# Batch 0 of a Fourier mixing and gated feed-forward kernel: the mean-frequency row on four column tiles, another order of the first loads, and the places and steps at which the weights are prepared

## The chip, the cores and the metric

The kernel runs on one core of one Trainium2 chip. The metric is the device time in microseconds (us); the median of three runs before is 1972.15 us (1970.73 to 1973.31).

## The reference

`x` is 8 batches of 3008 positions of 256 features, float32. Each batch goes through a two-dimensional Fourier transform of which the real part is kept; every position then goes through a gated feed-forward layer. The three weights arrive as 64-bit floats.

```python
def _attn_ref(x) -> np.ndarray:
    X = np.fft.fft(x, axis=1)
    X = np.fft.fft(X, axis=2)
    return X.real.astype(np.float32)
...
def _moe_ref(x, w_gate, w_val, w_out) -> np.ndarray:
    gate = 1.0 / (1.0 + np.exp(-(x @ w_gate)))
    val = x @ w_val
    return (gate * val @ w_out).astype(np.float32)
```

## The kernel before, in words

**Transform over positions.** The symmetry of the real transform is used: `fold_ops` (L347) adds and subtracts mirrored rows of a batch, and TensorE multiplies the folded rows with a table of cosines or sines (tile `st`, six pieces `q` of 126 rows, halves by `load_table`). Each product group has an even and an odd sum, `ev` and `od`; ScalarE copies `ev` out (L439) and VectorE combines the two (`places`, L444 and L447) into one of three tiles with a column per frequency: `pk` (cosine part), `qk` (sine part), and for batch 0 `ek`, the part E of the one feature in the middle (column HD). In batch 0 that one column is broadcast to all 128 columns of the stationary operand, so that `ek` holds the same row 128 times (`seq_group` with `what` = 2). The other seven batches get E as rows in one go, from `e_sums` (L476): the product has 7 columns, four products stand side by side at 32-column positions of the array, and the rows go to memory (`ed`) and come back broadcast (`e_rows`, tile `ek`).

**Weights.** There are 18 pieces of 512 KB, 256 columns of the gate or value weight or 256 rows of the output weight, in the order `jobs` (L205). A piece is loaded by SyncE's queue into a "raw" place (`weight_load`), taken apart on ScalarE (`weight_parts`, L262 and L263, two operations), joined to float32 on VectorE and GpSimd (`weight_join`, L272, L273, L275, and L277 on GpSimd), and used (`weight_use`). A gate or value piece is multiplied on TensorE with the feature transform `dt` (`merge`, matmuls `ps`), and ScalarE copies the result to `G1`, `G2` (L298, L299); two small transfers put row 0 of `G2` into `ge` (L301). An output piece goes to `WO`; when all that a group `g` needs of it is there, three operations for forming sums of weight blocks are appended to the list `parts_` (`forms`, L304; sums L334 and L337 by `W_SUMS`, copies on ScalarE L341). They write the 15 forms of group `g` in `wf`. Group 0 is formed on GpSimd, groups 1 to 3 on VectorE.

**The main loop** (`for i in range(count)`, L792) runs over 576 steps, one for 128 hidden units of a chunk of 252 frequencies; 12 steps make a chunk. Within a step the code order is the order on every engine, and the engines keep their own order. In step `i`:

- `front_a(i)`: TensorE multiplies `G1` with `pk` into PSUM tile `pf` (4 rows of the trace), in the first N1 steps also `G2` with a tile whose row 0 is E (`e0`, 4 rows);
- `part(i)`: a copy `ae` of `pf`, doubled, on ScalarE (L548); for N1 <= i < 12 instead two operations on VectorE that add E times `ge` (L551);
- `gate_a(i-1)`, `gate_b(i-1)`: sigmoid (ScalarE L567), difference (VectorE L572 or L569), product (VectorE L584), sigmoid (ScalarE L585), product (VectorE L586), and sums of blocks on GpSimd (L590);
- then, if `parts_` holds anything, its first operation, and the joins, parts and uses of weights that the two lists near the end (`pre`, `use`) give for this step; if `parts_` was empty, its first operation comes after them;
- from step 5 on `back((i-5)//3, (i-5)%3)`: 5 products with the forms in `wf` (matmuls `po`, 10 rows). `PRODUCTS` names the form of each: the third product of part 0 needs form 6, the fourth form 10; the first product of part 1 needs form 4. Group 1 is first used in step 8, group 2 in step 11, group 3 in step 14;
- `front_b(i)`: TensorE multiplies `G2` with `qk` into the same `pf` (4 rows).

From step 12 on, E enters by ScalarE's `seed` (L532), which writes `ek` times `ge` to the next `pf`.

Of the kernel before, what the change touches and what calls it, by code (L numbers as in the profile page):

```python
# [7 lines left out]
F32 = mybir.dt.float32  # L8
# [36 lines left out]

NQ = 6
NP = 126  # L50
HP = 64
# [3 lines left out]
              (15, 4, 6, 1)),  # L55
          2: ((11, 8, 11, 0), (12, 8, 12, 0), (9, 5, 9, 0), (10, 10, 5, 0), (16, 2, 11, 0),
              (16, 9, 16, 0))}
W_SUMS = (((1, 3), (5,), 1, 6), ((6, 7), (0, 2), 0, 8), ((4,), (8, 9), 0, 10), ((6,), (2, 3), 1, 12),
          ((0, 2), (1, 3), 0, 14), ((0,), (7,), 1, 16))
W_COPIES = ((2, -1), (0, 1), (4, 1), (5, 1))  # L60

PRODUCTS = ((0, 12), (1, 11), (4, 6), (6, 10), (2, 13), (5, 4), (13, 0),
# [15 lines left out]
def kernel(  # L78
# [10 lines left out]
    nc = tc.nc  # L89
    B, _, _, _, D = xf.shape  # L90
    F = moe_w_gate.shape[1]
    P = 128
# [102 lines left out]
    def table_again():  # L195

        ST[0] = const.tile([P, 2, NQ, NE + NO], F32, name="st", tag="st")
        for t in range(2):
# [3 lines left out]


    assert NPR == 6
    jobs = [(0, 0), (1, 0), (0, 1), (1, 1), (2, 0), (0, 2), (1, 2), (2, 1), (0, 3), (1, 3), (0, 4), (2, 2),  # L205
            (1, 4), (0, 5), (1, 5), (2, 3), (2, 4), (2, 5)]
    RAW, WS = {}, {}
    shared = {}
    KEEP = 10
# [1 line left out]
    def weight_load(j):  # L211


        w, c = jobs[j]
        src = (moe_w_gate, moe_w_val, moe_w_out)[w]
        src = src[2 * c * P : 2 * (c + 1) * P, :] if w == 2 else src[:, c * WC : (c + 1) * WC]
        src = src.rearrange("(c p) f -> p c f", p=P)

        def some(n, pool, tag):

            if tag not in shared:
                shared[tag] = pool.tile([P, n * WC], F32, name=f"w{tag}", tag=tag)
            return shared[tag]

        def home(j):

            if j in (0, 1, 2, 3, 5):
                if j > 2:
                    ws = some(5, pqp, "qk")[:, (j // 5) * 2 * WC : (j // 5 + 1) * 2 * WC]
                    return sp.tile([P, 4 * WC], F32, name="raw", tag="sf"), ws  # L230
                t = hp.tile([P, 6 * WC], F32, name="raw", tag="h")
                return t[:, 0 : 4 * WC], t[:, 4 * WC :]
            if j in (4, 6, 9):
                t = wf[:, {4: 1, 6: 2, 9: 3}[j]].rearrange("p m n -> p (m n)")
                return t[:, 0 : 4 * WC], t[:, 4 * WC : 6 * WC]
            t = some(10, cp, "c")
            if j == 7:
                raw = pqp.tile([P, 4 * WC], F32, name="raw", tag="pk")
                return raw, t[:, 6 * WC : 8 * WC]
            return t[:, 0 : 4 * WC], t[:, 4 * WC : 6 * WC]  # L240

        if j < KEEP:
            raw, ws = home(j)
        else:
            both = some(24, xp, "x4").rearrange("p (i n) -> p i n", n=2 * WC)
            r, i = (j - KEEP) % 3 * 2, 6 + (j - KEEP) % 6
            raw, ws = both[:, r : r + 2].rearrange("p a n -> p (a n)"), both[:, i]
        raw = raw.bitcast(I32).rearrange("p (c f w) -> p c f w", c=2, w=2)
        ws = ws.rearrange("p (c f) -> p c f", c=2)
        WS[j] = ws  # L250
        if src.dtype == F32:
            nc.sync.dma_start(out=ws, in_=src)
        else:
            RAW[j] = raw
            nc.sync.dma_start(out=raw.rearrange("p c f w -> p c (f w)"), in_=src.bitcast(I32))
# [48 lines left out]
    def forms(g):  # L304
# [1 line left out]
        w = [WO[f // 2].rearrange("p f (a h j) -> p f h a j", h=2, j=TB)[:, f % 2]  # L306
             for f in range(3 * g, 3 * g + 3)]
        f = wf[:, g].rearrange("p m (a j) -> p m a j", j=TB)
        engine = nc.vector if g else nc.gpsimd

        def one(i):
            return w[i // 2][:, i % 2] if i < 6 else f[:, i - 6]

# [14 lines left out]
        def sums(lo, hi):  # L328
            for x, y, op, to in W_SUMS[lo:hi]:
                n = max(len(x), len(y))  # L330
                a, b = blocks(x, n), blocks(y, n)
                op = (ALU.subtract, ALU.add)[op]
                if a is not None and b is not None:
                    engine.tensor_tensor(f[:, to - 6 : to - 6 + n], a, b, op=op)  # L334
                else:
                    for i in range(n):
                        engine.tensor_tensor(f[:, to - 6 + i], one(x[i % len(x)]), one(y[i % len(y)]), op=op)  # L337

        def copies():
            for i, (a, sign) in enumerate(W_COPIES):  # L340
# [6 lines left out]
    def fold_ops(b, nq):  # L347
# [58 lines left out]
            first(pool, 2, 3, qs[1])  # L406
            ops += [lambda: half1(qs[0]), lambda: half2(qs[1])]
        for blk, (v, r) in enumerate(parts):
            W[b, blk] = (v[:, :, 0:HD], r[:, :, 0:HD],
                         v[:, :, HD : HD + 1].to_broadcast([v.shape[0], NQ, P]))  # L410
        return ops


# [40 lines left out]

    def seq_start(b):
        PQE[b] = [pqp.tile([P, NK + 1], F32, name=name, tag=name) for name in ("pk", "qk")]
        if not b:
            PQE[b].append(op.tile([P, NK + 1], F32, name="ek", tag="os"))
        for t in PQE[b]:
            nc.vector.memset(t[:, NK:], 0.0)  # L460

# [11 lines left out]
        tt(x8[:, :, 1], x8[:, :, 0], x8[:, :, 2], op=ALU.add)  # L473
        tt(x8[:, :, 3], x8[:, :, 0], x8[:, :, 2], op=ALU.subtract)

    def e_sums():  # L476


        ps = bank("pe", 0)
        m = B - 1  # L480
        at_ = lambda blk, par: slice((2 * blk + par) * TB, (2 * blk + par) * TB + m)
        for q in range(0, NQ, 2):
            for blk in range(2):
                c0, n = ((0, NE), (NE, NO))[blk]
                for par in range(2):
                    mm(ps[at_(blk, par), 0:n], x8[:, :, 1 + 2 * blk, q + par],
                       ST[0][0:NP, 0, q + par, c0 : c0 + n], q == 0, q == NQ - 2)
        er = op.tile([P, NK + 1], F32, name="er", tag="os")[0:m]
        nc.vector.memset(er[:, NK:], 0.0)
        a = evp.tile([P, NE], F32, name="a", tag="a")[0:m]  # L490
        e1 = evp.tile([P, NE], F32, name="a", tag="a")[0:m]
        nc.scalar.copy(a, ps[at_(0, 1), 0:NE])
        nc.scalar.copy(e1[:, 0:NO], ps[at_(1, 0), 0:NO])

        def rest():
            places(er, 0, True, a, ps[at_(0, 0), 0:NE])
            nc.scalar.copy(a[:, 0:NO], ps[at_(1, 1), 0:NO])  # L497
            places(er, 1, False, e1[:, 0:NO], a[:, 0:NO])
            nc.scalar.dma_start(out=ed[1:], in_=er)
        return rest  # L500


# [17 lines left out]
        nc.sync.dma_start(out=EK[i // NFT], in_=ed[b : b + 1, k0 : k0 + n].to_broadcast([P, n]))  # L520

    PF, AP, Z = {}, {}, {}
    N1 = 5

    def seed(i):

# [16 lines left out]
    def part(i):  # L543

        pqe, ks, n, f, _ = cut(i)
        AP[i] = app.tile([P, 2, CH], F32, name="ae", tag="ae")[:, :, 0:n]
        if not N1 <= i < NFT:
            nc.scalar.activation(AP[i], PF[i], AF.Copy, scale=2.0)  # L548
            return
        for g in range(2):  # L550
            nc.vector.scalar_tensor_tensor(out=AP[i][:, g], in0=pqe[2][:, ks],  # L551
                                           scalar=ge[:, g, f : f + 1], in1=PF[i][:, g],
                                           op0=ALU.mult, op1=ALU.add)

# [131 lines left out]
    for j in range(2):  # L686
        weight_load(j)
    load_x(0)
    for _ in load_table(0, NQ // 2):
        pass  # L690
    for j in range(2, 5):
        weight_load(j)
    sines = load_table(1, NQ // 2)
    next(sines)
    for j in range(5, 7):
        weight_load(j)
    next(sines)
    for j in range(7, KEEP):
        weight_load(j)

    def weight_round(*js):
# [11 lines left out]

    e0 = shared["qk"][:, 4 * WC : 4 * WC + CH]
    nc.gpsimd.memset(e0, 0.0)
    other = {(0, 0): (4, None), (0, 1): (4, None), (0, 2): (0, 1), (1, 2): (2, 3)}
    cos = [seq_group(0, blk, what, other.get((blk, what))) for blk in range(2) for what in (0, 2)]
    for i, f in enumerate(fold_ops(0, NQ // 2)):
        f()
        for sums, _, _ in cos:  # L720
            sums(*range(i * NQ // 2, (i + 1) * NQ // 2))
    sin = [seq_group(0, blk, 1, other.get((blk, 1))) for blk in range(2)]
    for i in range(2):
        for sums, _, _ in sin:
            sums(*range(i * NQ // 2, (i + 1) * NQ // 2))
    evacuate = [then for _, then, _ in cos + sin]
    for then, js in zip(evacuate, ((2, 3), (4,), (5,), (6,), (7,), (8,))):
        weight_round(*js)
        then()()
    nc.scalar.dma_start(out=ed[0:1], in_=PQE[0][2][0:1])  # L730
    nc.vector.tensor_copy(e0[0:1], PQE[0][2][0:1, 0:CH])
    weight_parts(9)
    for j in range(KEEP, KEEP + 3):
        weight_load(j)
    weight_use(2)

# [5 lines left out]


    pre, use = {}, {}
    for j, i in enumerate((0, 1, 2, 3, 4, 5, 6, 7, 9), 9):
        if i:
            pre.setdefault(i - 1, []).append(lambda j=j: weight_parts(j))
        pre.setdefault(i, []).insert(0, lambda j=j: weight_join(j))
        if KEEP <= j < len(jobs) - 3:
            at(i, lambda j=j: weight_load(j + 3))  # L750
    for j, i in enumerate((0, 0, 1, 2, 0, 3, 4, 5, 4, 6, 7, 8, 8, 8, 11), 3):
        use.setdefault(i, []).append(lambda j=j: weight_use(j))
    at(N1 - 1, lambda: nc.vector.tensor_copy(PQE[0][1][0:1, 0:CH], PQE[0][2][0:1, 0:CH]))


    i0 = NFT
# [7 lines left out]
    for i, f in enumerate(mirror_tables()):  # L764
        at(2 * i0 - 2 + i, f)
    at(3 * i0, e_fold)
    at(3 * i0 + 4, lambda: e_sums()())
    at(3 * i0 + 6, table_again)
    for i in range(i0, count, i0):
        at(i - 8, lambda i=i: e_rows(i))  # L770

    for b in range(B - 1):
        s0 = b * per
# [97 lines left out]
```

## Time and profile before

| | |
|---|---|
| median of three runs | 1972.15 us |
| profiled execution, its own time | 1973.76 us |
| its span, first to last instruction | 1972.0 us |
| TensorE busy | 1935.8 us, 98% |
| VectorE, ScalarE, GpSimd busy | 1511.7, 1339.5, 1625.0 us |
| mean granted TensorE clock | 0.995 |
| steps 0, 12 and 16 begin (`pf` from `pk`) | 49.02, 107.91, 120.76 us |

A timeline line gives the start, the duration (of all merged instructions together), engine, line, operation, output and inputs, shapes, and in brackets the idle time before it and what ended it. A table of stretches gives the length, then the busy time and the number of instructions of each engine, TensorE's granted clock, the share of the transfer engines and their rate. `PEld` is TensorE's weight load, which lies beside its matmuls. A float32 product is two rows of the trace.

### The profile page before, as it was taken

The page shows a single profiled execution, that of the slowest core. Times are in us where ns is not written, and L with a number is a line of the kernel's source. Part 1 is how long each engine was busy: PE and PEld are TensorE (multiplying, and loading weights), DVE is VectorE, ACT ScalarE, POOL GpSimd, SP SyncE. Part 2 cuts the span into 40 slices and gives each one's busy share as a digit, 9 for nine tenths or more (in the row PEclk, how much of TensorE's full clock was granted, in tenths as well). Part 3 has the DMA queues.
Part 4 walks back from the last instruction along what each step waited for, and adds up shares of the span by engine and source line. Part 5 has one row for each costly group of instructions (what it writes and reads, how often), then busy time and mean ns, then how long its engine had stood idle before and what let it go on. Part 6 is the DMA issues. An engine that isn't in the chain of part 4 may idle for free.

```text
span 1972.0 us, 34403 instructions
## 1 busy us (share of the span) xinstructions
PE 1935.8 (98%) x11252; PEld 1792.4 (91%) x11252; DVE 1511.7 (77%) x3170; ACT 1339.5 (68%) x3108; POOL 1625.0 (82%) x2843
## 2 busy tenths in 40 slices
PE   6999999999999999999999999999999999999997
PEld 4889889999999899998999989999899999999997
DVE  6888778886787677786778867787678776777777
ACT  3567657766777577775777757777577766777775
POOL 3779888997889788996889868998688996777776
PEclk9999999999999999999999999999999999999999
DMA  8363412212022121212012021211210110011011
GB/s 271 86 134 94 138 52 85 51 22 78 14 51 54 17 76 17 72 31 78 14 28 78 14 78 25 47 48 24 78 19 14 21 20 14 14 20 22 14 19 27
DMA packets 171584, 101.41 MB, mean 51 GB/s; under 512 B 133904, under 2 KB 163218, under 8 KB 168602
## 3 DMA queue, kind: packets, MB, share of 16 engines
q1 hardware_dynamic: 169434, 98.64, 20.6%
q8 instruction: 90, 1.47, 0.3%
q10 hardware_dynamic: 1940, 0.56, 0.1%
q14 instruction: 88, 0.72, 0.1%
q0 software_dynamic: 32, 0.00, 0.0%
HBM read 74.45 MB, written 50.18 MB: 63 GB/s over the span
## 4 chain that ended last, share of the span: by engine, by line
PE 95%; DMA 2%; DVE 2%; ACT 1%; issue 0%; POOL 0%; SPq 0%; ACTq 0%; DVEq 0%; POOLq 0%
PE pf L129 49%; PE po L129 41%; PE ev L129 4%; DMA st<-in_stab_dram 1%; PE ps L129 1%; DMA ge<-G 1%; PE od L129 0%; DMA raw<-in_moe_w_val_dram 0%; DMA xr<-in_xf_dram 0%; DVE c L637 0%; DVE ae L551 0%; DVE wf L337 0%; DVE wx L273 0%; ACT z L585 0%; DVE wx L275 0%
## 5 line engine op out<-in xcount | busy, mean ns | idle before, releaser
L590 POOL TENSOR_TENSOR sf<-h 128x168 f32<-128x168 f32 (+1 forms) x960 | 548.8, 590 | 221.6 <-DVE h L586 221.6
L590 POOL TENSOR_TENSOR sf<-h,sf 128x168 f32<-128x168 f32 (+1 forms) x1152 | 657.2, 590 | 60.5 <-DVE h L586 60.5
L129 PE MATMUL pf<-qk,G 128*128 128x252 f32 (+1 forms) x2304 | 582.4, 375 | 3.1 <-DVE ae L551 2.0
L129 PE MATMUL pf<-pk,G 128*128 128x252 f32 (+1 forms) x2304 | 583.4, 376 | 0.0
L586 DVE TENSOR_TENSOR h<-z 128x252 f32<-128x252 f32 (+1 forms) x576 | 299.1, 519 | 356.9 <-ACT z L585 356.6
L532 ACT ACTIVATE pf<-ek,ge 128x252 f32<-128x252 f32 (+1 forms) x1128 | 531.4, 471 | 18.4
L129 PE MATMUL po<-sf,wf 128*128 128x168 f32 (+1 forms) x3072 | 530.1, 305 | 0.0
L548 ACT ACTIVATE ae<-pf 128x504 f32<-128x504 f32 (+1 forms) x569 | 335.0, 589 | 245.6 <-PE pf L129 245.5
L637 DVE TENSOR_TENSOR c<-c 128x168 f32<-128x168 f32 (+1 forms) x949 | 484.3, 541 | 5.5 <-ACT c L614 0.3
L129 PEld LDWEIGHTS pf<-pk,G 128*128 128x128 f32 x2304 | 436.7, 190 | 52.6 <-issue 2.3
L129 PEld LDWEIGHTS po<-sf,wf 128*128 128x128 f32 x3072 | 472.8, 190 | 8.3
L129 PE MATMUL po<-h,wf 128*128 128x168 f32 (+1 forms) x2688 | 477.2, 306 | 1.7 <-ACT a L497 1.6
L129 PEld LDWEIGHTS po<-h,wf 128*128 128x128 f32 x2688 | 428.8, 191 | 19.0 <-ACT a L497 2.0
L129 PEld LDWEIGHTS pf<-qk,G 128*128 128x128 f32 x2304 | 410.2, 190 | 29.2 <-DVE ae L551 2.6
L572 DVE TENSOR_TENSOR z<-ae,pf 128x504 f32<-128x504 f32 (+1 forms) x569 | 377.4, 663 | 21.5 <-ACT h L567 20.9
L567 ACT ACTIVATE h<-pf 128x252 f32<-128x252 f32 (+1 forms) x576 | 217.9, 378 | 164.0 <-PE pf L129 152.9
L585 ACT ACTIVATE z<-z 128x252 f32<-128x252 f32 (+1 forms) x576 | 231.1, 401 | 80.3 <-DVE z L572 60.1
L584 DVE TENSOR_TENSOR h<-h,pf 128x252 f32<-128x252 f32 (+1 forms) x576 | 231.9, 403 | 0.0
L590 POOL TENSOR_TENSOR sf<-sf 128x168 f32<-128x168 f32 (+1 forms) x192 | 111.3, 580 | 15.1
L590 POOL TENSOR_TENSOR sf<-sf,h 128x168 f32<-128x168 f32 (+1 forms) x192 | 106.6, 555 | 0.0
L129 PE MATMUL ev<-st,x 63*128 63x376 f32 (+4 forms) x372 | 98.0, 414 | 8.3 <-DVE x L364 7.8
L129 PEld LDWEIGHTS ev<-st,x 63*128 63x128 f32 (+1 forms) x372 | 66.4, 187 | 36.1 <-DVE x L364 8.2
(120 smaller groups left out, 861.9 us busy)
## 6 DMA issues: line engine op xcount, KB each, us to landing
x<-xr SPq DMA_DIRECT2D x14, 1536.0 KB
out_dram<-os SPq DMA_DIRECT2D x380, 56.0 KB
xr<-in_xf_dram SPq DMA_DIRECT2D x14, 768.0 KB
xr<-in_xf_dram SPq DMA_DIRECT2D x35, 256.0 KB
ek<-ed SPq DMA_DIRECT2D x39, 126.0 KB
out_dram<-os SPq DMA_DIRECT2D x288, 7.0 KB
st<-in_stab_dram SPq DMA_DIRECT2D x4, 1111.9 KB
x<-in_xf_dram SPq DMA_DIRECT2D x2, 1512.0 KB
```

What stands on the lines that cost most here:

```text
L129: nc.tensor.matmul(o, l, r, start=start, stop=stop, skip_group_check=True)
L532: nc.scalar.activation(PF[i][:, g], EK[i // NFT], AF.Copy, scale=ge[:, g, f : f + 1])
L548: nc.scalar.activation(AP[i], PF[i], AF.Copy, scale=2.0)
L567: nc.scalar.activation(H[p][:, fh, 0:n], PF[i][:, 0], AF.Sigmoid)
L572: nc.vector.tensor_tensor(z[:, :, ::-1], AP.pop(i), PF[i], op=ALU.subtract)
L584: nc.vector.tensor_tensor(h[:, fh, 0:n], h[:, fh, 0:n], PF.pop(i)[:, 1], op=ALU.mult)
L585: nc.scalar.activation(z[:, 0], z[:, 0], AF.Sigmoid)
L586: nc.vector.tensor_tensor(h[:, fh, n:], z[:, 0], z[:, 1], op=ALU.mult)
L590: nc.gpsimd.tensor_tensor(block(p, dst), block(p, a), block(p, b), op=(ALU.subtract, ALU.add)[op])
L637: engine.tensor_tensor(t[:, dst * R : (dst + 1) * R], *v, op=(ALU.subtract, ALU.add)[op])
```

## The change

1. **E of batch 0.** `e_sums` gets the number of rows, the column and the batch as arguments and is used for batch 0 too, with one row: 12 products at four column positions take the place of the 12 with the broadcast column. The row goes to memory, and `e_rows(0)` brings it back, broadcast, for VectorE's E part of steps 8 to 11. All later `e_rows` are issued two steps sooner (`i - 10`).
2. **Loads.** The sines' first half is loaded directly behind the cosines, the second half after one weight piece; pieces 3 to 9 follow. The order of pieces (`jobs`) changes: gate and value pieces 0 to 2 come first, then the first two output pieces.
3. **Places.** From piece 10 on there are five raw places where there were three (two of them in a second tile of pool `cp`), and five pieces are loaded ahead of the loop.
4. **Before the loop** only pieces 2 to 4 are prepared (it was 2 to 8); the later joins and uses move into the loop by the two lists.
5. **Forms.** Group 0 is formed on VectorE; `W_SUMS` is in another order, so that the first two operations give what part 0 of `back` needs, and the third gives form 4 for part 1.
6. **N1** goes from 5 to 8: TensorE adds E in three more steps, and VectorE in three fewer.

```diff
-W_SUMS = (((1, 3), (5,), 1, 6), ((6, 7), (0, 2), 0, 8), ((4,), (8, 9), 0, 10), ((6,), (2, 3), 1, 12),
-          ((0, 2), (1, 3), 0, 14), ((0,), (7,), 1, 16))
+W_SUMS = (((1, 3), (5,), 1, 6), ((0,), (7,), 1, 16), ((6,), (2, 3), 1, 12), ((6, 7), (0, 2), 0, 8),
+          ((4,), (8, 9), 0, 10), ((0, 2), (1, 3), 0, 14))
...
-    jobs = [(0, 0), (1, 0), (0, 1), (1, 1), (2, 0), (0, 2), (1, 2), (2, 1), (0, 3), (1, 3), (0, 4), (2, 2),
-            (1, 4), (0, 5), (1, 5), (2, 3), (2, 4), (2, 5)]
+    jobs = [(w, c) for c in range(3) for w in range(2)] + [(2, 0), (2, 1), (0, 3), (1, 3)]
+    jobs += [(0, 4), (1, 4), (2, 2), (0, 5), (1, 5), (2, 3), (2, 4), (2, 5)]
...
-            r, i = (j - KEEP) % 3 * 2, 6 + (j - KEEP) % 6
-            raw, ws = both[:, r : r + 2].rearrange("p a n -> p (a n)"), both[:, i]
+            r, ws = (j - KEEP) % 5, both[:, 6 + (j - KEEP) % 6]
+            if r < 3:
+                raw = both[:, 2 * r : 2 * r + 2].rearrange("p a n -> p (a n)")
+            else:
+                if r == 3:
+                    shared["more"] = cp.tile([P, 10 * WC], F32, name="wm", tag="c")
+                raw = shared["more"][:, (r - 3) * 4 * WC : (r - 2) * 4 * WC]
...
-        engine = nc.vector if g else nc.gpsimd
...
-            W[b, blk] = (v[:, :, 0:HD], r[:, :, 0:HD],
-                         v[:, :, HD : HD + 1].to_broadcast([v.shape[0], NQ, P]))
+            W[b, blk] = v[:, :, 0:HD], r[:, :, 0:HD], v[:, :, HD : HD + 1]
...
-    N1 = 5
+    N1 = 8
...
-            nc.vector.scalar_tensor_tensor(out=AP[i][:, g], in0=pqe[2][:, ks],
+            nc.vector.scalar_tensor_tensor(out=AP[i][:, g], in0=EK[i // NFT],
...
-    for _ in load_table(0, NQ // 2):
-        pass
-    for j in range(2, 5):
-        weight_load(j)
+    list(load_table(0, NQ // 2))
     sines = load_table(1, NQ // 2)
     next(sines)
-    for j in range(5, 7):
-        weight_load(j)
+    weight_load(2)
     next(sines)
-    for j in range(7, KEEP):
+    for j in range(3, KEEP):
         weight_load(j)
...
-    cos = [seq_group(0, blk, what, other.get((blk, what))) for blk in range(2) for what in (0, 2)]
+    cos = [seq_group(0, blk, 0, (2 * blk + 1, 2 * blk + 2)) for blk in range(2)]
...
+    e_row = e_sums(1, lambda blk, q: W[0, blk][2][:, q], 0)
...
-    for then, js in zip(evacuate, ((2, 3), (4,), (5,), (6,), (7,), (8,))):
-        weight_round(*js)
+    for _, then, _ in cos:
         then()()
-    nc.scalar.dma_start(out=ed[0:1], in_=PQE[0][2][0:1])
-    nc.vector.tensor_copy(e0[0:1], PQE[0][2][0:1, 0:CH])
-    weight_parts(9)
-    for j in range(KEEP, KEEP + 3):
+    e_row = e_row()
+    weight_round(2)
+    nc.vector.tensor_copy(e0[0:1], e_row[:, 0:CH])
+    for j, (_, then, _) in zip((3, 4), sin):
+        weight_round(j)
+        then()()
+    weight_parts(5)
+    for j in range(KEEP, KEEP + 5):
         weight_load(j)
     weight_use(2)
...
-    for j, i in enumerate((0, 1, 2, 3, 4, 5, 6, 7, 9), 9):
+    for j, i in enumerate((0, 1, 2, 2, 3, 4, 5, 6, 6, 7, 8, 9, 10), 5):
...
-    for j, i in enumerate((0, 0, 1, 2, 0, 3, 4, 5, 4, 6, 7, 8, 8, 8, 11), 3):
+    for j, i in enumerate((0, 1, 2, 3, 3, 4, 5, 6, 7, 7, 8, 9, 10, 10, 12), 3):
         use.setdefault(i, []).append(lambda j=j: weight_use(j))
-    at(N1 - 1, lambda: nc.vector.tensor_copy(PQE[0][1][0:1, 0:CH], PQE[0][2][0:1, 0:CH]))
+    at(N1 - 1, lambda: nc.vector.tensor_copy(PQE[0][1][0:1, 0:CH], e_row[:, 0:CH]))
...
+    e_rows(0)
     for i in range(i0, count, i0):
-        at(i - 8, lambda i=i: e_rows(i))
+        at(i - 10, lambda i=i: e_rows(i))
```

More of the change, by code (lines that the diff above doesn't have):

```diff
@@ L333, in sums @@
                 if a is not None and b is not None:
-                    engine.tensor_tensor(f[:, to - 6 : to - 6 + n], a, b, op=op)
+                    nc.vector.tensor_tensor(f[:, to - 6 : to - 6 + n], a, b, op=op)
                 else:
                     for i in range(n):
-                        engine.tensor_tensor(f[:, to - 6 + i], one(x[i % len(x)]), one(y[i % len(y)]), op=op)
+                        nc.vector.tensor_tensor(f[:, to - 6 + i], one(x[i % len(x)]), one(y[i % len(y)]), op=op)
         def copies():
@@ L456, in seq_start @@
         PQE[b] = [pqp.tile([P, NK + 1], F32, name=name, tag=name) for name in ("pk", "qk")]
-        if not b:
-            PQE[b].append(op.tile([P, NK + 1], F32, name="ek", tag="os"))
         for t in PQE[b]:
@@ L474, in e_fold, with e_sums @@
         tt(x8[:, :, 3], x8[:, :, 0], x8[:, :, 2], op=ALU.subtract)
-    def e_sums():
+    def e_sums(m, column, b):
         ps = bank("pe", 0)
-        m = B - 1
         at_ = lambda blk, par: slice((2 * blk + par) * TB, (2 * blk + par) * TB + m)
@@ L485, in e_sums @@
                 for par in range(2):
-                    mm(ps[at_(blk, par), 0:n], x8[:, :, 1 + 2 * blk, q + par],
+                    mm(ps[at_(blk, par), 0:n], column(blk, q + par),
                        ST[0][0:NP, 0, q + par, c0 : c0 + n], q == 0, q == NQ - 2)
[L488 to L493, printed above, removed]
-        def rest():
+        def rest():
+            er = op.tile([P, NK + 1], F32, name="er", tag="os")[0:m]
+            nc.vector.memset(er[:, NK:], 0.0)
+            a = evp.tile([P, NE], F32, name="a", tag="a")[0:m]
+            e1 = evp.tile([P, NE], F32, name="a", tag="a")[0:m]
+            nc.scalar.copy(a, ps[at_(0, 1), 0:NE])
+            nc.scalar.copy(e1[:, 0:NO], ps[at_(1, 0), 0:NO])
             places(er, 0, True, a, ps[at_(0, 0), 0:NE])
@@ L498, in rest @@
             places(er, 1, False, e1[:, 0:NO], a[:, 0:NO])
-            nc.scalar.dma_start(out=ed[1:], in_=er)
+            nc.scalar.dma_start(out=ed[b : b + m], in_=er)
+            return er
         return rest
@@ L715 @@
     nc.gpsimd.memset(e0, 0.0)
-    other = {(0, 0): (4, None), (0, 1): (4, None), (0, 2): (0, 1), (1, 2): (2, 3)}
-    cos = [seq_group(0, blk, what, other.get((blk, what))) for blk in range(2) for what in (0, 2)]
+    cos = [seq_group(0, blk, 0, (2 * blk + 1, 2 * blk + 2)) for blk in range(2)]
     for i, f in enumerate(fold_ops(0, NQ // 2)):
@@ L721 @@
             sums(*range(i * NQ // 2, (i + 1) * NQ // 2))
-    sin = [seq_group(0, blk, 1, other.get((blk, 1))) for blk in range(2)]
+    e_row = e_sums(1, lambda blk, q: W[0, blk][2][:, q], 0)
+    sin = [seq_group(0, blk, 1, (None, 1 if blk else None)) for blk in range(2)]
     for i in range(2):
@@ L725 @@
             sums(*range(i * NQ // 2, (i + 1) * NQ // 2))
-    evacuate = [then for _, then, _ in cos + sin]
-    for then, js in zip(evacuate, ((2, 3), (4,), (5,), (6,), (7,), (8,))):
-        weight_round(*js)
+    for _, then, _ in cos:
         then()()
-    nc.scalar.dma_start(out=ed[0:1], in_=PQE[0][2][0:1])
-    nc.vector.tensor_copy(e0[0:1], PQE[0][2][0:1, 0:CH])
-    weight_parts(9)
-    for j in range(KEEP, KEEP + 3):
+    e_row = e_row()
[6 more added lines that the diff above has]
+    for j in range(KEEP, KEEP + 5):
         weight_load(j)
@@ L748 @@
         pre.setdefault(i, []).insert(0, lambda j=j: weight_join(j))
-        if KEEP <= j < len(jobs) - 3:
-            at(i, lambda j=j: weight_load(j + 3))
-    for j, i in enumerate((0, 0, 1, 2, 0, 3, 4, 5, 4, 6, 7, 8, 8, 8, 11), 3):
+        if KEEP <= j < len(jobs) - 5:
+            at(i, lambda j=j: weight_load(j + 5))
+    for j, i in enumerate((0, 1, 2, 3, 3, 4, 5, 6, 7, 7, 8, 9, 10, 10, 12), 3):
         use.setdefault(i, []).append(lambda j=j: weight_use(j))
-    at(N1 - 1, lambda: nc.vector.tensor_copy(PQE[0][1][0:1, 0:CH], PQE[0][2][0:1, 0:CH]))
+    at(N1 - 1, lambda: nc.vector.tensor_copy(PQE[0][1][0:1, 0:CH], e_row[:, 0:CH]))
     i0 = NFT
@@ L766 @@
     at(3 * i0, e_fold)
-    at(3 * i0 + 4, lambda: e_sums()())
+    at(3 * i0 + 4, lambda: e_sums(B - 1, lambda blk, q: x8[:, :, 1 + 2 * blk, q], 1)())
     at(3 * i0 + 6, table_again)
+    e_rows(0)
     for i in range(i0, count, i0):
-        at(i - 8, lambda i=i: e_rows(i))
+        at(i - 10, lambda i=i: e_rows(i))
     for b in range(B - 1):
```

## The prediction

> **What bounds the kernel now.** I read the page first, then the table of stretches for the first 250 us, the timeline by engine and the chain of waits. The page's slices, about 49 us each:
>
> ```profile
> PE   6999999999999999999999999999999999999997
> PEclk9999999999999999999999999999999999999999
> ```
>
> TensorE is the bound from the third slice on, so what the first 120 us lose or win passes to the end one for one. Those stretches:
>
> ```profile
> 70.00:80.00 10.00, 7.95 (x38) 6.17 (x36) 9.63 (x18) 5.28 (x16) 6.96 (x10) 1.00 0.53 163
> 80.00:90.00 10.00, 9.43 (x50) 8.44 (x51) 9.56 (x19) 3.58 (x11) 8.99 (x12) 1.00 0.22 54
> 90.00:100.00 10.00, 10.00 (x58) 9.26 (x56) 9.21 (x20) 4.28 (x13) 7.21 (x11) 1.00 0.19 45
> 100.00:110.00 10.00, 8.00 (x37) 7.34 (x36) 9.45 (x20) 4.23 (x13) 7.33 (x12) 0.83 0.54 179
> ```
>
> The third busy column is VectorE: 9.2 to 9.6 of 10 us. In steps 5 to 11 VectorE is as tight as TensorE. The timeline of TensorE:
>
> ```profile
> 102.15 1.12 PE L129 MATMUL pf<-qk,G 128*128 128x252 f32 x4 [2.00 <-DVE ae L551]
> 103.11 1.50 PE L129 MATMUL pf<-pk,G 128*128 128x252 f32 x4
> ...
> 114.16 1.01 PE L129 MATMUL pf<-pk,G 128*128 128x252 f32 x4
> 115.01 1.94 PE L129 MATMUL po<-h,wf 128*128 128x168 f32 x10
> 116.78 1.01 PE L129 MATMUL pf<-qk,G 128*128 128x252 f32 x4
> ```
>
> A wait of 2.00 us, then four rows in 1.50 us instead of 1.01. At 115.01 (step 14, part 0 of group 3) ten products take 1.94 instead of 1.59. The chain says why:
>
> ```profile
> 113.91 0.50 DVE h L586
> 114.41 1.09 DVE wf L337 x2
> 115.51 0.56 DVE wf L334
> 116.07 0.04 issue
> 116.11 0.84 PE po L129 x4
> ```
>
> This is the most useful view here: forms that stand in the code of step 13 run on VectorE 3.3 us after step 13 began (111.04, timeline), behind that step's L586, and TensorE, already in step 14, waits for them.
>
> **What the Trainium skill says.** "TensorEngine Tiling (Array Packing)", Overview: with at most 32 stationary columns, four products can run side by side. The trace agrees: `e_sums` of the other batches takes
>
> ```profile
> 198.98 2.09 PE L129 MATMUL pe<-st,x 126*7 126x377 f32 x24
> ```
>
> where 24 full-width rows at 0.317 us would take 7.6. "SBUF — State Buffer", on the shared port pair: a VectorE operation with two SBUF inputs or in a two-port mode excludes GpSimd for its length. It agrees: L272 takes 0.43 us with GpSimd idle (5.34) and 0.76 beside it (79.64). "TensorE: Matmul & The Clock Gate", Part 1: after an idle window of some 3.4 us the array runs at half rate for such a window. Here 2.0 us of waiting were enough (clock 0.83 in the stretch 100 to 110).
>
> **Part by part.**
>
> *E row.* Removes 24 full rows, 7.6 us, adds 24 tiled ones, 2.05: TensorE -5.6 us, on the path only if the sines are there. `places` costs the same four VectorE operations (0.54 each) and three copies. The row's store puts a wait on ScalarE for the last `places`; behind it stands all of piece 2 (`weight_parts`). `e_rows(0)` has over 30 us: free.
>
> *Sines sooner.* Now 11,056 KB lie ahead of and in the second half, which lands at 42.92 (TensorE waits 0.52 for it). In the new order 9,008 KB. By the landings seen (6,784 KB at 25.85, 9,432 KB at 36.35) that is about 34.9. First halves of the cosine groups as now, 21.39 to 27.1; second halves bound by VectorE and GpSimd folding (26.9, 28.9), to 30.9; E row to 32.9; sines 24 rows of 0.317 to 40.5. Sums end at 40.5 instead of 47.0: **-6.5 us**. Pieces 3 and 4 land later, about 36.6 and 38.5.
>
> *Before the loop.* VectorE: E row until 36.6 (0.54-us operations, and ScalarE copies between), piece 2 to 39.6 (0.43 + 0.43 + 0.69 after 0.67 on ScalarE), `e0` 40.3, piece 3 41.9, `qk` 43.0, piece 4 44.8, `qk` 45.9. TensorE: merge 2 at 41.1 when GpSimd is done (1.29 after 39.7), 1.73 long; step 0 begins at 43.1 (now 49.02) and step 1 at 47.3 (now 54.34): **-7 us**.
>
> *N1.* TensorE gets 3 x 0.85 = +2.55 us in steps 5 to 7; VectorE loses 6 x 0.43 = -2.6, ScalarE gets 3 x 0.59.
>
> *Group 0 on VectorE.* Six sums leave GpSimd (0.73 each; 4.4 us) and cost VectorE five at 0.42 and one at 0.28, 2.4, up to 0.77 each beside GpSimd. So VectorE's work is about level; but joins 5 to 8 (4 x 1.55 to 2.3) move behind the loop's start. They are hidden while steps are long (4.3 us to step 4, 5.7 with a merge and `back`), and not later.
>
> *Five raw places.* Loads 10 to 14 can start at 40.5 and land by some 57; piece 10 is wanted in step 3. A load waits for the join that frees its place on SyncE's queue, with `ge` transfers behind it; load 17 goes at about 82, `ge` of piece 11 at 83. Free, or 1 us. The earlier `e_rows` pass nothing that is late: free.
>
> *Later uses.* Gate and value of chunk c are merged one step ahead instead of two. Then ScalarE's G copies (0.75, behind two pieces' parts, 2.7 us in steps 1 and 5) are late: I count waits of 0.4 (step 2), 0.4 (step 5) and 1.1 (step 6), 1 for the lack of a merge in step 3 and 0.9 in step 4, where `pf` waits for VectorE.
>
> *Forms just in time.* This decides. Output piece 12 is used in step 7 (now 4), 16 in 10 (now 8), 17 in 12 (now 11). One operation is popped per step, so group 1 forms in steps 7, 8, 9, group 2 in 10, 11, 12, group 3 in 13, 14, 15. `back` wants them in steps 8 and 9, 11 and 12, 14 and 15: form 6 stands in the second operation, form 4 in the third, both popped in the very step that needs them. The new order of sums gives back one step, the later uses take two or three. From the trace a step's sums start 3.3 us after the step's beginning (the chain above: sigmoid, difference, product, sigmoid, product come first) and the first one ends at 3.7 (L334, 0.42). TensorE wants it after 0.85 (part 1) or 0.85 + 2 x 0.285 = 1.42 (part 0). So the waits in the steps without a merge are: step 12 2.9, step 14 2.4, step 15 3.0 us. In steps 8 and 9 a merge of 1.73 covers some, but L551 comes first on VectorE (+0.85): 1.2 and 1.6. In step 11 VectorE still has join 17 and sums of step 10 ahead: about 5.
>
> Begin of steps, from these terms (join 1.9 us, between both ends):
>
> | step | now | after |
> |---|---|---|
> | 0 | 49.0 | 43.1 |
> | 4 | 67.2 | 60.7 |
> | 8 | 89.7 | 84.3 |
> | 10 | 97.7 | 96.7 |
> | 12 | 107.9 | 108.2 |
> | 14 | 114.2 | 117.6 |
> | 16 | 120.8 | 129.2 |
>
> Steps 12 to 16: 4 x 3.13 + 8.3 = 20.8 after, 12.85 now. So **+8.4** at step 16. The clock: the waits of 2.4 to 5 us may each bring a half-rate window (lost 0 to 1.7, part of it hidden, since the next wait is VectorE's); I take one, +1.5. After step 16 nothing differs; the stop at the other batches' `e_sums` (step 40) stays.
>
> **Sum.** The profiled execution (1973.76, its span 1972.0) is 1.6 above the median; +9.9 gives 1983.7 against it and **1982.0** against the median 1972.15.
>
> **Rivals.**
>
> *Faster: the prologue's gain outweighs.* If VectorE kept up (joins at 1.55, no backlog in steps 8 to 11), TensorE's own work gives step 12 at 95.8 (43.1 + 12 x 1.7 + 8 x 0.85 + 9 x 1.73 + 7 x 1.425); with 20.8 after it step 16 at 116.6: -4.2, 1968. The point from which it decides: step 12 before 100.0. For it: TensorE's work falls by 3.0 us and all data are earlier. Against: VectorE above 9.2 of 10 in these stretches and no less work after.
>
> *Level: waits smaller.* Step 12 at about 101, as with a backlog of half; -7 at step 12 and +8: 1973.
>
> *Half clock each time.* Five windows at 1.7 on top of +8.4: 1989.
>
> **How the numbers follow.** Forecast 0.62, half clock 0.12 (both slower), level 0.15, faster 0.11. What a measurement of this kernel can tell from no change is 0.2%, 3.9 us. So slower 0.74, same 0.15, faster 0.11. The range 1970 to 1990 takes in the level case, the join at 1.55 to 2.3 us (step 12 at 103 to 113) and most of the clock case; left out are the faster case and the worst clocks.
>
> **What would show it.** Right: sums end near 40.5; step 0 near 43; waits of `po` for VectorE's `wf` (L334, L337) in steps 8, 9, 11, 12, 14, 15, together some 16 us, and step 16 near 129. Wrong: step 12 before 104, or `po` products of part 1 in steps 12 and 15 that start within 1 us of the `pf` rows ahead of them; then the forms were not the path. If the sines still end past 43, the loads were not the limit that I took them for.

## The result, and the profile after

The changed kernel takes 1991.97 us (median of 4 runs, 1989.13 to 1994.87) against 1972.55 us for the kernel before in the same comparison: ratio 1.010, 95% interval 1.0082 to 1.0117. It is slower by 19.4 us. The forecast was slower by 9.9 us with a range up to 1990; the direction and most of the mechanism held, the size did not.

The profiled execution has a span of 1989.6 us, 17.6 more than before. All of it lies in the first 140 us: step 16 begins at 138.34 us instead of 120.76, which is 17.58 later. (The medians are 1.8 us further apart, because the profiled execution before took 1.2 us more than its median here and that of the changed kernel 0.6 us less.) In the page's slices this is a little more idle time in the second and third slice and a clock below full in the third:

```profile
PE   6879999999999999999999999999999999999997
PEclk9989999999999999999999999999999999999999
```

What TensorE waited for longest in the first 150 us (total, times, longest), from the view of the waits:

```profile
PE po L128 <- DVE wf L337: 16.0, 6, 4.5
PE ps L128 <- POOL raw L281: 9.1, 2, 8.6
PE ev L128 <- DVE x L367: 6.5, 1, 6.5
PE pf L128 <- DVE h L584: 1.6, 1, 1.6
```

The first line is new. The second (all but 0.5 us) and the third are the start, ahead of the first sums, and stand in the kernel before as well (8.4 and 7.8 us). Six waits of `po` for forms in `wf`, 16.0 us together. The timeline of TensorE shows where, here in steps 8 and 9:

```profile
87.18 0.73 PE L128 MATMUL po<-h,wf 128*128 128x168 f32 x4
91.28 2.05 PE L128 MATMUL po<-h,wf 128*128 128x168 f32 x6 [3.37 <-DVE wf L337]
93.13 1.89 PE L128 MATMUL pf<-qk,G 128*128 128x252 f32 x4
94.81 1.89 PE L128 MATMUL pf<-pk,G 128*128 128x252 f32 x4
96.49 2.27 PE L128 MATMUL ps<-wx,dt 128*128 128x256 f32 x8
99.47 0.55 PE L128 MATMUL po<-h,wf 128*128 128x168 f32 x2 [0.72 <-DVE wf L337]
```

Two products (four rows), then the wait for form 6, then rows at half pace: four `pf` rows take 1.89 us where they took 1.01 before. The chain of waits through the same stretch:

```profile
88.63 0.77 DVE ae L551 x2
89.41 0.60 DVE z L572
90.03 0.42 ACT z L585
90.47 0.42 DVE h L586
90.89 0.35 DVE wf L337
91.24 0.04 issue
91.28 2.05 PE po L128 x6
```

It reads as foretold: E part, difference, sigmoid, product, and only then the form that TensorE has been waiting for since about 87.9. The clock is in the table of stretches (last but two column):

```profile
80.00:90.00 10.00, 7.92 (x42) 7.00 (x40) 9.68 (x17) 3.87 (x11) 7.35 (x8) 1.00 0.26 68
90.00:100.00 10.00, 8.00 (x25) 6.70 (x26) 7.53 (x16) 4.21 (x11) 5.16 (x8) 0.66 0.01 0
100.00:110.00 10.00, 6.56 (x39) 5.94 (x37) 9.60 (x18) 3.17 (x12) 6.78 (x9) 1.00 0.38 116
110.00:120.00 10.00, 6.27 (x21) 5.54 (x22) 3.98 (x9) 2.36 (x6) 4.94 (x9) 0.72 0.45 155
120.00:130.00 10.00, 7.90 (x43) 7.26 (x43) 5.11 (x12) 5.55 (x15) 3.93 (x8) 0.94 0.13 46
130.00:140.00 10.00, 7.32 (x32) 6.44 (x31) 4.45 (x9) 3.71 (x9) 4.51 (x10) 0.83 0.31 97
```

TensorE is busy 6.3 to 8.0 of 10 us from 80 to 140, and in four of these stretches it did not have its full clock. In finer stretches the clock is at 0.50 from 90.4 to 97.2, 110.9 to 114.3, 117.7 to 121.1 and 134.8 to 138.2: five half-rate windows of 3.4 us, the first two in a row. The kernel before has one such window in its loop, from 103.5 to 106.9, behind the wait of 2.00 us.

Begin of steps (the `pf` rows from `pk`) and span in the profiled executions, us:

| kernel | step 0 | 4 | 8 | 12 | 16 | span |
|---|---|---|---|---|---|---|
| before | 49.02 | 67.17 | 89.73 | 107.91 | 120.76 | 1972.0 |
| changed | 42.98 | 59.37 | 84.61 | 114.45 | 138.34 | 1989.6 |
| waits filled | 42.35 | 58.73 | 83.97 | 109.94 | 130.72 | 1981.8 |
| forms at once | 42.76 | 59.15 | 87.96 | 113.38 | 127.76 | 1978.9 |
| two forms first | 43.00 | 59.39 | 87.33 | 112.25 | 125.64 | 1976.8 |
| forms at once, sines late | 50.73 | 67.12 | 96.62 | 122.29 | 136.90 | 1988.0 |
| forms spread | 44.82 | 61.21 | 86.45 | 109.05 | 123.71 | 1974.9 |
| forms spread, N1 = 12 | 42.61 | 59.00 | 84.40 | 104.94 | 119.18 | 1970.6 |
| before, N1 = 12 | 48.15 | 66.28 | 88.41 | 106.03 | 118.88 | 1970.3 |

In every row the difference to before at step 16 and that in the span agree within 0.2 us: nothing after step 16 plays a part.

### The profile page after: what moved, and what is told of

It is laid out like the page before. It is cut to its first block, busy times and chain, and to the rows that moved or that the text cites. A ratio compares the mean times of both kernels' runs of the same rounds, so it can differ in the third digit from the quotient of the medians.

```text
span 1989.6 us, 34421 instructions
## 1 busy us (share of the span) xinstructions
PE 1940.7 (98%) x11264; PEld 1796.1 (90%) x11264; DVE 1515.6 (76%) x3170; ACT 1342.5 (67%) x3112; POOL 1624.1 (82%) x2837
## 4 chain that ended last, share of the span: by engine, by line
PE 95%; DVE 3%; ACT 1%; DMA 1%; issue 0%; SPq 0%; ACTq 0%; DVEq 0%
PE pf L128 49%; PE po L128 41%; PE ev L128 4%; DMA x<-in_xf_dram 1%; PE od L128 1%; DVE h L586 0%; PE ps L128 0%; ACT z L585 0%; DVE wf L337 0%; PE pe L128 0%; DVE wx L279 0%; DVE c L637 0%; DVE ae L551 0%; DVE wx L276 0%; DVE z L572 0%
```

## The experiments

Each run was timed beside the kernel before, whose median was 1974.00 us beside numbers 1 to 4, 1974.10 beside 5 to 8 and 1973.74 beside 9 and 10; beside the changed kernel it was 1972.55. So a distance to the changed kernel that is taken from the medians is uncertain by some 1.5 us, and the ratios to before are the firmer figures.

**1. All form operations of a group at once.**

```diff
-        for f in [parts_.pop(0)] + todo if parts_ else todo + [lambda: parts_ and parts_.pop(0)()]:
-            f()
+        for f in todo:
+            f()
+        while parts_:
+            parts_.pop(0)()
```

> Changed kernel, but all three form operations of a group run at the end of the step in which its last output piece is used, instead of one a step. Theory (the forms come just in time, and each wait brings a half-rate window): the waits of the po products for VectorE's forms in steps 9, 11, 12, 14 and 15 vanish (12.7 us together in the changed kernel), 1 to 2.5 us stay in step 8, at most two half-rate windows stay; step 16 begins at 115 to 122 instead of 138.3, time 1968 to 1976. Rival (VectorE has too much to do in steps 5 to 12 in any order, the wait only moves to the E part or to pf): 1985 or more.

Measured: 1980.99 us, ratio to before 1.0031 (1.0013 to 1.0049). That is 11 us better than the changed kernel and between the two expectations. The longest waits of TensorE from 14 to 150 us behind the one for the first sums:

```profile
PE pf L128 <- DVE h L584: 4.8, 1, 4.8
PE po L128 <- DVE wf L337: 3.9, 1, 3.9
PE pf L128 <- DVE ae L551: 2.6, 2, 1.5
```

The form waits fall from 16.0 to 3.9 us, but bursts of forms make VectorE late with other things: `pf` waits 4.8 us for the product that frees its bank (step 5, behind group 0's six sums), and four half-rate windows remain (two around step 5, two in steps 11 and 12). So the forms were the cause of the larger part, and the rival, a full VectorE, is right for a part.

**2. Two form operations first.** The first two operations of a group run in the step of use, the third in the next step, and piece 17 is used in step 11.

```diff
-        for f in [parts_.pop(0)] + todo if parts_ else todo + [lambda: parts_ and parts_.pop(0)()]:
+        for f in [parts_.pop(0)] + todo if parts_ else todo + [lambda: parts_ and (parts_.pop(0)(), parts_.pop(0)())]:
...
-    for j, i in enumerate((0, 1, 2, 3, 3, 4, 5, 6, 7, 7, 8, 9, 10, 10, 12), 3):
+    for j, i in enumerate((0, 1, 2, 3, 3, 4, 5, 6, 7, 7, 8, 9, 10, 10, 11), 3):
```

> Changed kernel, but of a new group the first two form operations run together at the end of the step of use, the third in the next step, and output piece 17 is used in step 11 instead of 12. Every form is then made one step or more ahead of its product. Theory: as with all three at once, 1968 to 1976, with 1 to 2.5 us of waiting left in step 8. Rival (VectorE's load in any order): 1985 or more. It differs from the run with all three at once only if the length of a burst of forms matters: by under 3 us.

Measured: 1978.36 us, 1.0018 (1.0011 to 1.0025), 2.4 us above the range expected. The largest wait is not in step 8 but in step 11 (3.4 us), where VectorE comes to group 2's sums behind the join of piece 17; `pf` in step 5 still waits 3.0 us. Three half-rate windows remain, two in steps 5 and 6 and one behind the wait in step 11.

**3. The waits filled with products by zeros.** The forms come as late as in the changed kernel; TensorE runs extra products ahead of the waiting one, so that it isn't idle. The stationary tile is zero, so they add nothing to the sums.

```diff
+    FILL = {(1, 2): 10, (1, 5): 2, (2, 2): 14, (2, 5): 8, (3, 2): 6, (3, 5): 8}
...
+            for _ in range(FILL.get((p, at_), 0)):
+                mm(PO[t][:, j * R : (j + 1) * R], e0[:, 0:P], block(p, hb), False, False)
...
+    at(N1 - 1, lambda: nc.gpsimd.memset(e0, 0.0))
```

> Changed kernel with extra products by a stationary tile of zeros (128x168 moving, 0.285 us each) that TensorE runs ahead of the waiting product: 10, 2, 14, 8, 6 and 8 of them in steps 8, 9, 11, 12, 14 and 15, a little shorter than the waits. The forms come as late as before. Theory (the half-rate windows after the waits cost a term of their own, 7.9 us by the busy time inside them): no half-rate window after 85 us, the waits' ends stay where VectorE puts them, time 1981 to 1986. Rival (the half rate is hidden under the next wait, all is the waits): 1989 to 1993.

Measured: 1983.64 us, 1.0048 (1.0033 to 1.0063), inside the expectation: 8.3 us faster than the changed kernel (9.8 if each is taken against its own kernel before) with 48 products more. The stretches of this run:

```profile
80.00:90.00 10.00, 9.65 (x55) 8.80 (x54) 9.49 (x17) 4.59 (x13) 6.93 (x8) 1.00 0.19 53
90.00:100.00 10.00, 9.11 (x52) 8.27 (x51) 9.64 (x19) 4.15 (x11) 8.05 (x12) 1.00 0.04 2
100.00:110.00 10.00, 9.48 (x61) 8.96 (x60) 8.35 (x17) 2.73 (x9) 6.13 (x9) 1.00 0.59 191
110.00:120.00 10.00, 9.60 (x58) 8.90 (x57) 4.53 (x11) 5.35 (x15) 4.50 (x9) 1.00 0.31 108
120.00:130.00 10.00, 9.20 (x58) 8.51 (x57) 6.48 (x14) 4.72 (x11) 5.41 (x12) 1.00 0.05 18
130.00:140.00 10.00, 10.00 (x59) 9.39 (x58) 6.65 (x15) 7.25 (x17) 5.17 (x10) 1.00 0.91 328
```

The clock is 1.00 throughout, and step 16 begins 7.6 us sooner (138.34 to 130.72). Of this, 0.6 us was there at step 0 and at step 8 (84.61 to 83.97), ahead of the first filled wait; the other 7.0 us arise from step 8 to step 16 and are the price of the half rate. The forms come as late as before: from the beginning of the step to the end of the wait it is 6.67 us in the changed kernel and 6.62 here in step 8, 6.08 and 6.10 in step 11, and between 3.68 and 3.69 in both in steps 12, 14 and 15. What this run is behind the kernel before at step 16, 10.0 us, is the late forms with the rest of the change.

**4. Sines late, with all forms at once.**

```diff
+    for j in range(2, 5):
+        weight_load(j)
     sines = load_table(1, NQ // 2)
     next(sines)
-    weight_load(2)
+    for j in range(5, 7):
+        weight_load(j)
     next(sines)
-    for j in range(3, KEEP):
+    for j in range(7, KEEP):
```

> As the run with all three form operations at once, but the sines' halves are loaded in the places that they had before (behind pieces 2 to 4, and behind 5 and 6). Theory (the loads ahead of the sines set the end of the first sums): the sums end at 43 to 47 us instead of 40.5, step 0 begins 1.5 to 4 us later, and of that 1 to 4 us reach the end. Rival (hidden by VectorE's load in steps 5 to 11): the same time within 1 us.

Measured: 1992.37 us (1987.95 to 1995.03 in four runs), 1.0089 (1.0067 to 1.0111), 11.4 us above the run with forms at once; in the spans 9.1. More than either theory said. TensorE waits for the sines:

```profile
35.55 1.50 PE L128 MATMUL ev<-st,x 126*128 126x377 f32 x4 [1.07 <-DMA st<-in_stab_dram]
...
43.41 0.90 PE L128 MATMUL ev<-st,x 126*128 126x377 f32 x2 [3.83 <-DMA st<-in_stab_dram]
44.15 2.22 PE L128 MATMUL od<-st,x 126*128 126x377 f32 x4
46.16 1.46 PE L128 MATMUL ev<-st,x 126*128 126x376 f32 x2
47.41 1.75 PE L128 MATMUL od<-st,x 126*128 126x376 f32 x4
```

The second half lands at 43.41, near the 42.92 of before; the last rows then run at half rate (clock 0.50 from 44.6 to 48.1), and step 0 begins 8.0 us later. Of the 8.0 us, 1.9 were there before the sines were needed (the E row's products begin at 32.40 and 30.54), because in this execution the first sums ran at half rate for longer; about 6.1 are the sines and what follows their waits. The lead at step 0 does pass to the end here: 8.0 us at step 0 are 9.1 at step 16. Both runs have the same work in the loop; that this is why the lead is kept is argued, not tested.

**5. Forms spread.** Group 0 one operation a step as in the changed kernel, groups 1 to 3 in two operations (copies and four sums, then two sums), piece 17 joined in step 11.

```diff
+        if g:
+            return [lambda: (copies(), sums(0, 4)), lambda: sums(4, 6)]
         return [lambda: (copies(), sums(0, 2)), lambda: sums(2, 4), lambda: sums(4, 6)]
...
-    for j, i in enumerate((0, 1, 2, 2, 3, 4, 5, 6, 6, 7, 8, 9, 10), 5):
+    for j, i in enumerate((0, 1, 2, 2, 3, 4, 5, 6, 6, 7, 8, 9, 11), 5):
```

> Changed kernel with each form made a step or more ahead, and spread out: group 0 one operation a step as in the changed kernel, groups 1 to 3 in two operations (copies and the first four sums, then the last two), and piece 17 joined in step 11 instead of 10. Theory (late forms and the half-rate windows that they cause are the loss; bursts of forms on VectorE give some back as waits for pf): better than two at once for all groups, 1972 to 1977. Rival (VectorE is full in steps 5 to 11 whatever the order of the forms): 1978 to 1982, as with all or two at once.

Measured: 1975.11 us, 1.0005 (0.9997 to 1.0014), inside the expectation: level with before, and 16.9 us better than the changed kernel by an edit of when the forms and the join of piece 17 are made. The form waits are down to 1.9 us, and no half-rate window is left in the loop. VectorE is busy 9.5 to 9.6 of 10 us from 60 to 100. (In the profiled execution the first sums ran longer at half rate, which is why step 0 stands 2 us later in the table.)

**6. The same with N1 = 12.** TensorE adds E in all twelve steps.

```diff
-    N1 = 8
+    N1 = 12
```

> As the spread forms, and N1 is 12: TensorE adds E in all twelve steps of the first chunk, so VectorE loses the eight L551 (3.7 us) of steps 8 to 11 and TensorE gets 4 x 0.85 = 3.4 us. Theory (VectorE is the bound there): 1 to 4 us faster than the spread forms with N1 = 8. Rival (TensorE is the bound there): 3.4 us slower.

Measured: 1972.35 us, 0.9989 (0.9981 to 0.9997): 2.8 us better, so VectorE, not TensorE, set steps 8 to 11. In its profiled execution there is one half-rate window, around step 5 (65.7 to 69.2), which number 5 does not have.

**7. Forms spread, group 0's sums on GpSimd** (N1 = 8).

```diff
-                    nc.vector.tensor_tensor(f[:, to - 6 : to - 6 + n], a, b, op=op)
+                    (nc.vector if g else nc.gpsimd).tensor_tensor(f[:, to - 6 : to - 6 + n], a, b, op=op)
```

> As the spread forms with N1 = 8, but the sums of group 0 are on GpSimd, as before the change. Theory (VectorE's load in steps 3 to 5 makes pf late in step 5: 1.7 us of waiting in the changed kernel): 1 to 3 us faster than the spread forms. Rival (GpSimd has the joins and block sums of the same steps and is as full): slower by 1 to 4 us, with waits for joined weights or for form 6 in step 5.

Measured: 1975.35 us, 1.0004 (0.9996 to 1.0013), the same as on VectorE. Step 5 begins sooner (64.17 us; 65.86 in the changed kernel), and a wait comes back on the other engine, in step 6:

```profile
PE po L128 <- POOL wf L337: 1.4, 1, 1.4
```

Each expectation was right about the waits and wrong about the time; the engine of group 0 makes no difference that was measured.

**8. The kernel before with N1 = 8** (`N1 = 5` to `N1 = 8`).

> The kernel before with N1 = 8 as its only edit. TensorE gets 3 x 0.85 = 2.55 us in steps 5 to 7, VectorE loses as much. If VectorE sets those steps in the kernel before (busy 9.2 to 9.6 of 10): 1970 to 1973, level or a little faster. If TensorE sets them: 1975.

Measured: 1973.42 us, 0.9998 (0.9990 to 1.0006): level, 0.4 us above the range given for VectorE, but without the 2.55 us more that TensorE would have cost. In the traces steps 5 to 7 take 17.97 us (18.28 in the kernel before).

**9. N1 = 12 and group 0 on GpSimd** (edits 5, 6 and 7 together).

> As the spread forms with N1 = 12, but the sums of group 0 are on GpSimd. Step 5 should begin 1 to 3 us sooner, as it did with N1 = 8; theory: with VectorE relieved in steps 8 to 11 as well, 1 to 2 us of it reach the end, 1970 to 1971.5. Rival: GpSimd's block sums come later in turn and the wait moves to form 6 in step 5 and to the block products, 1972 to 1974.

Measured: 1972.93 us, 0.9993 (0.9985 to 1.0001): not better than number 6; the rival's range.

**10. The kernel before with N1 = 12** (`N1 = 5` to `N1 = 12`).

> The kernel before with N1 = 12 as its only edit. VectorE loses 14 L551 (6 us) in steps 5 to 11, TensorE gets 7 x 0.85 = 6 us. If the gain of the spread forms with N1 = 12 is N1's alone, this is as fast, 1971 to 1973. If it needs the earlier start of the loop, where TensorE has room, this is slower than before: 1974 to 1976.

Measured: 1971.92 us, 0.9989 (0.9983 to 0.9996): as fast as number 6 against its own kernel before (0.9989 both). So the gain of number 6 is no larger than that of N1 alone, and its early loop start is worth nothing by step 16: the lead over the kernel before with the same N1 is 5.5 us at step 0 (42.61 to 48.15), 7.3 at step 4, 4.0 at step 8, 1.1 at step 12 and -0.3 at step 16.

## Why the prediction was right in direction and wrong in size

**Right: the earlier sums.** The last sine rows end at 40.63 (40.5 was said), step 0 begins at 42.98 (43.1), step 4 at 59.37 (60.7), step 8 at 84.61 (84.3). The order of the loads is needed for it: with the sines late (number 4), step 0 is 8.0 us later, about 6.1 of them by the sines, and the whole gain over the kernel before is 6.0, so the narrower E row shows no gain without the loads. What the loads would gain with the E row at full width was not run. The sum has one slip that decides nothing: by the landings that it names, the second half of the sines is due at 34.7, not 34.9.

**Right: forms just in time.** The sum of the six waits was put at 1.2 + 1.6 + 5 + 2.9 + 2.4 + 3.0 = 16.1 us and is 16.0. They stand in steps 8, 9, 11, 12, 14 and 15: 3.37, 0.72, 4.50, 2.67, 2.10, 2.68. Steps 12, 14 and 15, which were read from the chain of the kernel before, are within 0.35 us, and the form is ready 3.7 us after the step's beginning, as was said (3.69 in steps 12 and 15). That the total fits to 0.1 us is luck: step 8 is 2.2 us over, and steps 9 and 11 are 0.9 and 0.5 under. In step 8, one operation of the join and a sum of two blocks took 1.51 and 1.26 us (L276 at 83.70, L337 at 86.84) where GpSimd's joins ran, and a copy of the E row into `qk` (L751, 0.62 us at 88.02) was not in the sum at all, so VectorE came to the forms later than a join of 1.9 us allowed. In step 9 the half rate hides a part: with the waits filled, 1.5 us lie there between the merge's end and the form (95.06 to 96.53). The prediction's own terms give 1.4 and 2.0 for steps 8 and 9, not 1.2 and 1.6, and 129.0, not 129.2, for step 16; neither slip decides anything. Numbers 1, 2 and 5 take lateness away by the times of the forms (2 and 5 also of piece 17) and win 11.0, 13.6 and 16.9 us; the half-rate windows that go with it are in these figures.

**Wrong: the clock.** The step that failed is "I take one, +1.5": one half-rate window, partly hidden. There were five, and the run with filled waits prices them at 7.0 us from step 8 to step 16. By the busy time inside them it would be 7.8 us: TensorE works 5.96, 3.25, 2.99 and 3.42 us of these windows, half of which is lost. So only 0.8 us was hidden, where the prediction had expected a part of each loss to vanish in the next wait. The two traces show why: in steps 8, 11, 12, 14 and 15 the form comes as late after the beginning of its step with the half rate as without it (number 3), but the slow rows stand between the end of a wait and the beginning of the next step, and so move all that follows. The case stood among the rivals ("half clock each time", 1989, 0.12), with the right count of windows and the wrong chance. Without the clock the sum holds: step 16 was put at +8.4 us, and the run without half-rate windows has +10.0. The rest of the distance, 1.6 us, is no more than what steps 8 and 9 are over (14.94 us in that run, 12.4 in the prediction's table).

**The rivals.** "Faster, the prologue's gain outweighs" failed at its own point: step 12 at 114.45, not before 100.0; nor is it near the 101 of "level". Even with the forms in time and VectorE relieved (number 6), step 12 begins at 104.94. So VectorE doesn't keep up in any order tried. It is busy 9.2 to 9.7 of 10 us from 60 to 100 in number 6, and joins 5 to 8, which ran before the loop, stand in it now; that these joins are the reason is argued, not tested. The lead of 5 to 7 us at steps 0 to 4 is spent by step 16 (number 10).

**N1 and group 0.** N1 = 8 was taken as level, 2.55 us from one engine to the other; number 8 agrees. Group 0 on VectorE was taken as about level; number 7 agrees.

**Open.** Against the kernel before with the same N1, number 6 loses 5.8 us from step 0 to step 16. In the traces 3.0 of them are waits of TensorE (4.3 us idle against 1.3), and about 1.7 is half of the 3.4 us that it works in the half-rate window around step 5; the rest is not placed, and no run moved the joins back to show what they cost. The five raw places were not run on their own either. In the trace the E row's 24 rows take 2.08 us (2.05 was said).

## What to carry to other kernels

When preparatory work is moved later in a program whose engines keep their order, look up in which step the consumer stands: an operation put into the very step that needs it runs behind that step's whole chain, here 3.3 us after the step's beginning. Price a wait of TensorE of about 2 us or more with the half-rate window that can follow it, as a term of its own and not as a rival; here five windows cost 7.0 us, a little under half of TensorE's busy time inside them. And a lead at the start is worth only what the rest of the path leaves of it: here N1 = 12 alone, which takes some 6 us (14 L551) from VectorE, made the kernel before as fast as the reworked start with the forms spread and the same N1.

## What the runs showed of the hardware that I had not expected

- Waits of 3.37, 4.50, 2.67 and 2.68 us were followed by half-rate windows, one of 2.10 us wasn't; in the kernel before one of 2.00 us was. In numbers 6 and 5 the same wait of 1.65 us stands ahead of step 5; in number 6 half rate followed (four rows in 1.87 us), in number 5 it didn't. So the length of the wait alone doesn't decide between 1.65 and 2.1 us.

```profile
65.50 1.87 PE L128 MATMUL pf<-pk,G 128*128 128x252 f32 x4 [1.65 <-DVE h L586]
...
67.72 1.12 PE L128 MATMUL pf<-pk,G 128*128 128x252 f32 x4 [1.65 <-DVE h L586]
```

- With products by a stationary tile of zeros in the waits (number 3) the clock stayed at 1.00 all through the loop: for the granted clock they counted as work, though they compute nothing.
- After the long wait of step 8 the half rate lasted 6.8 us, two windows, although TensorE was busy from 91.3 us on.
